# Four idle matmuls ahead of the second projection, in place of two ahead of the second and two ahead of the third

## The chip, the cores and the metric

The kernel runs on one NeuronCore of a Trainium2 chip. The metric is the device time of one execution in microseconds; the kernel before takes 975.07 us, the median of three runs (974.72 to 975.36).

## What is computed

Random-feature attention for 8 batches of 8 heads (576 tokens, 64 dimensions, 128 features), then a two-layer network with a softplus between (512 to 2048 to 512) over the 4608 tokens:

```python
def phi(x):
    proj = np.einsum('bhsd,md->bhsm', x, omega)
    sq = np.sum(x * x, axis=-1, keepdims=True) / 2.0
    h = proj - sq
    h = h - np.max(h, axis=-1, keepdims=True)
    return np.exp(h) / np.sqrt(m)
q_p, k_p = (phi(q_s), phi(k_s))
kv = np.einsum('bhsm,bhsd->bhmd', k_p, v)
z = np.sum(k_p, axis=2)
num = np.einsum('bhsm,bhmd->bhsd', q_p, kv)
den = np.einsum('bhsm,bhm->bhs', q_p, z)[..., None] + 1e-06
...
h = x @ w_in
g = np.maximum(h, 0.0) + np.log1p(np.exp(-np.abs(h)))
return (g @ w_out).astype(np.float32)
```

## The kernel before

The work is cut into *works*, one for each step on one engine: a load, the squares of a unit, its projection, its maxima, its bias, its exponentials, a product. A *unit* is one or two tiles of 128 tokens of a *quad* (four heads of one batch). The list `ORDER`, written out in the code, says in which order the works go to the engines, and each engine then runs its own part of that order strictly in a row; semaphores hold an instruction until what it reads has been made and what it overwrites has been read.

The change lies in the first microseconds, in the units of the first batch, keys first. One unit goes like this. SyncE issues its load (L664, tile `xk`). ScalarE squares it (L674; later GpSimd, L676) and VectorE sums the squares (L681). TensorE projects it on `omf` (L691): four float32 products on 64 rows each, of two of the heads in one bank and the other two in a second, which the profile shows as eight matmuls. VectorE takes the maxima of each bank (L739), and two short steps make the bias from maxima and squares (L746, L751). ScalarE makes the exponentials from the banks and the bias (L759), which frees the banks. The exponentials are the stationary side of the products with the values (L908, tile `kt`). In names such as `ppk_1_0_0` the first two numbers are the quad and the unit, the third the bank. The first five projections in their order on TensorE are 0_0, 1_0, 0_1, 1_1 and 0_2.

On VectorE the order of the units is interlaced: the bias of 0_0 (L751) stands behind the maxima of 1_0 (L739), and the bias of 1_0 behind the maxima of both banks of 0_1.

*Idle matmuls* are products whose result nobody reads. `fill` (L1779) makes n of them: each takes a 128x128 bfloat16 view of the unit matrix as weights and streams it four times, 512 columns, into a bank. Six, of a tile of zeros, stand at the start of TensorE's order, ahead of the first projection. The dictionary `early_` (L1784) gives for the works of mode "r" (the projections of the first batch), from the second on, how many idle matmuls go ahead of each; they write the first bank that the projection itself will write, so the projection waits until the last of them has been drained. A projection without idle matmuls ahead has no such wait. Later in the kernel there are no idle matmuls, and the order of the works doesn't depend on `early_`.

Of the kernel before, what the change touches and what calls it, by code (L numbers as in the profile page):

```python
# [464 lines left out]
def favor_softplus_kernel(ctx, tc, q0, k0, qx, kx, tx, vv, om, wi, wo, out):  # L465
# [49 lines left out]
    works, saves = [], []  # L515
# [1265 lines left out]
        for _ in range(n):  # L1781
            nc.tensor.matmul(t, x, x.unsqueeze(1).broadcast_to([P, 4, P]), start=True, stop=True)

    early_ = dict(zip([id(w) for w in works if w.mode == "r"][1:], (2, 2, 1, 1)))  # L1784
    with tc.manual_schedule():
        fill("at.0", 6, idle)
        out_, held = in_order(works, room)
# [107 lines left out]
```

## Time and profile before

| | |
|---|---|
| median of three runs | 975.07 us (974.72 to 975.36) |
| the profiled execution | 979.14 us |
| its span, first to last instruction | 977.4 us |
| TensorE busy | 967.2 us, 99% |
| VectorE busy | 783.2 us, 80% |
| ScalarE busy | 681.5 us, 70% |

All rows come from the one profiled execution. Times are microseconds from the start of its span. PE is the matmul side of TensorE and PEld its weight loads, DVE is VectorE, ACT ScalarE, POOL GpSimd. Each row of a timeline is a run of like instructions of one line; the number behind the start is the time from the start of the first to the end of the last, and what stands in brackets is how long the engine was idle ahead of it and what ended that. Matmuls overlap, so that the ends of one row and the start of the next can cross.

### The profile page before, as it was taken

To read this page: it belongs to the slowest core of one execution; us is meant where nothing else is said; L and a number is where in the kernel's file an instruction comes from. 1 tells how busy PE (TensorE), PEld (TensorE's weight loads), DVE (VectorE), ACT (ScalarE), POOL (GpSimd) and SP (SyncE) were. 2 spreads that over 40 slices of the span, in tenths; PEclk is the share of its full clock that TensorE was granted. 3 is DMA by queue.
4 is the path that set the end of the run, shared out by engine and by line. 5 is a ranking of instruction groups with operands and counts; after the bars stand their busy time and mean duration, and the time that the engine had idled before them with its cause. 6 is when DMAs were issued, how large, how long until landed. Compare 5 with 4: busy or idle time off the path is not lost.

```text
span 977.4 us, 17669 instructions
## 1 busy us (share of the span) xinstructions
PE 967.2 (99%) x5503; PEld 789.5 (81%) x5503; DVE 783.2 (80%) x2755; ACT 681.5 (70%) x1686; POOL 310.7 (32%) x282
## 2 busy tenths in 40 slices
PE   9999999999999999999999999999999999999998
PEld 6888888888788878888888887888888777888886
DVE  7999988887888788886988887888787778988610
ACT  6999976768576876877695677867586665766720
POOL 1344442323144341125442353333424212322100
PEclk9999999999999999999999999999999999999999
DMA  9877355444333433543343434432532511000002
GB/s 338 327 264 248 109 151 149 130 129 124 108 102 94 119 108 109 149 129 101 109 136 102 110 100 137 128 112 87 154 101 67 149 47 44 1 1 1 1 11 75
DMA packets 65116, 113.85 MB, mean 116 GB/s; under 512 B 18376, under 2 KB 38016, under 8 KB 65024
## 3 DMA queue, kind: packets, MB, share of 16 engines
q1 hardware_dynamic: 64720, 112.54, 36.8%
q8 instruction: 44, 0.72, 0.3%
q14 instruction: 48, 0.39, 0.1%
q10 hardware_dynamic: 304, 0.20, 0.1%
HBM read 85.68 MB, written 27.03 MB: 115 GB/s over the span
## 4 chain that ended last, share of the span: by engine, by line
PE 71%; DVE 2%; DMA 1%; issue 0%; ACT 0%; ACTq 0%; DVEq 0%
PE acc L1316 11%; PE acc L1317 11%; PE acc L1318 11%; PE h L1256 7%; PE h L1257 7%; PE h L1258 7%; PE pb L1596 3%; PE xp L1185 2%; PE pa L1596 2%; PE pc L1596 2%; PE ppk L716 2%; PE ppq L716 2%; PE kt L857 1%; PE ku L857 1%; DMA fdq<-flq 1%
## 5 line engine op out<-in xcount | busy, mean ns | idle before, releaser
L1316 PE MATMUL acc<-wo,gh 128*128 128x512 f32 x512 | 204.3, 399 | 0.0
L1317 PE MATMUL acc<-wo,gh 128*128 128x512 f32 x512 | 200.7, 392 | 0.0
L1318 PE MATMUL acc<-wo,gl 128*128 128x512 f32 x512 | 199.6, 390 | 0.0
L1256 PE MATMUL h<-xh,wi 128*128 128x512 f32 (+1 forms) x512 | 188.9, 369 | 0.0
L1257 PE MATMUL h<-xl,wi 128*128 128x512 f32 (+1 forms) x512 | 186.4, 364 | 0.0
L1258 PE MATMUL h<-xh,wi 128*128 128x512 f32 (+1 forms) x512 | 185.6, 363 | 0.0
L1279 POOL TENSOR_TENSOR gl<-u,gh 128x512 fp32r<-128x512 f32 (+1 forms) x75 | 88.9, 1186 | 227.9 <-ACT gh L1275 150.3
L1316 PEld LDWEIGHTS acc<-wo,gh 128*128 128x128 f32 x512 | 96.3, 188 | 23.1 <-issue 7.4
L1318 PEld LDWEIGHTS acc<-wo,gl 128*128 128x128 f32 x512 | 96.2, 188 | 21.0
L1256 PEld LDWEIGHTS h<-xh,wi 128*128 128x128 f32 x512 | 96.5, 188 | 18.3 <-DVE u L1271 1.5
L1262 ACT ACTIVATE u<-h 128x512 f32<-128x512 f32 (+1 forms) x128 | 70.7, 553 | 57.5 <-PE h L1258 41.9
L1258 PEld LDWEIGHTS h<-xh,wi 128*128 128x128 f32 x512 | 96.5, 188 | 15.7
L1317 PEld LDWEIGHTS acc<-wo,gh 128*128 128x128 f32 x512 | 96.6, 189 | 14.4
L1257 PEld LDWEIGHTS h<-xl,wi 128*128 128x128 f32 x512 | 96.7, 189 | 13.6
L1271 DVE SCALAR_TENSOR_TENSOR u<-h,u 128x512 f32<-128x512 f32 (+1 forms) x128 | 79.0, 617 | 28.8 <-ACT u L1268 26.8
L1265 ACT ACTIVATE u<-u 128x512 f32<-128x512 f32 (+1 forms) x128 | 75.3, 589 | 1.8
L1268 ACT ACTIVATE u<-u 128x512 f32<-128x512 f32 (+1 forms) x128 | 74.8, 585 | 1.8
L736 ACT ACTIVATE phk<-phk,smk 128x128 f32<-128x128 f32 x208 | 68.7, 393 | 4.4 <-DVE smk L751 4.1
L1094 DVE CUSTOM_DVE_ANT_0 junk<-phq,zb 128x128 uint8<-128x128 f32 (+1 forms) x228 | 68.7, 334 | 1.2 <-ACT phq L759 0.6
L1103 POOL TENSOR_TENSOR phq<-phq,dnq 128x512 f32<-128x512 f32 (+1 forms) x39 | 42.2, 1088 | 80.8 <-DVE dnq L1099 73.2
L736 ACT ACTIVATE phq<-phq,smq 128x128 f32<-128x128 f32 x194 | 62.5, 393 | 7.1 <-DVE smq L751 7.1
L731 DVE CUSTOM_DVE_ANT_0 phk<-ppk,phk 128x128 f32<-128x128 f32 x208 | 51.4, 285 | 12.6 <-ACT phk L726 11.2
(213 smaller groups left out, 2020.3 us busy)
## 6 DMA issues: line engine op xcount, KB each, us to landing
xk<-kx SPq DMA_DIRECT2D x28, 512.0 KB, 3.5
xq<-qx SPq DMA_DIRECT2D x28, 512.0 KB, 3.7
fdq<-flq SPq DMA_DIRECT2D x28, 512.0 KB, 3.2
qq<-fdq SPq DMA_DIRECT2D x112, 128.0 KB, 3.1
rawi<-wi SPq DMA_DIRECT2D x16, 512.0 KB, 6.9
rawo<-wo SPq DMA_DIRECT2D x16, 512.0 KB, 6.2
out<-o SPq DMA_DIRECT2D x32, 256.0 KB, 3.9
v<-vv SPq DMA_DIRECT2D x14, 576.0 KB, 4.3
```

The lines of the kernel that those rows point to most:

```text
L736: nc.scalar.activation(x, x, AF.Exp, bias=b["sm"][:, 2, c : c + 1])
L1256: nc.tensor.matmul(b["h"], wh, xh[:, cc, t], start=cc == 0, stop=False)
L1257: nc.tensor.matmul(b["h"], wh, xl[:, cc, t], start=False, stop=False)
L1258: nc.tensor.matmul(b["h"], wl, xh[:, cc, t], start=False, stop=cc == NCC - 1)
L1262: nc.scalar.activation(b["u"], b["h"], AF.Abs)
L1265: nc.scalar.activation(b["u"], b["u"], AF.Exp, scale=-1.0)
L1268: nc.scalar.activation(b["u"], b["u"], AF.Ln, bias=1.0)
L1271: nc.vector.scalar_tensor_tensor(b["u"], b["h"], 0.0, b["u"], ALU.max, ALU.add)
L1279: (nc.vector if e == "DVE" else nc.gpsimd).tensor_tensor(b["gl"], b["u"], b["gh"].bitcast(F32), ALU.subtract)
L1316: nc.tensor.matmul(dst, gh, w2[fc][:, 0, c], start=start, stop=False, **kw)
L1317: nc.tensor.matmul(dst, gh, w2[fc][:, 1, c], start=False, stop=False, **kw)
L1318: nc.tensor.matmul(dst, gl, w2[fc][:, 0, c], start=False, stop=stop, **kw)
```

## The change

The four numbers of `early_` are those of the second to the fifth projection.

```diff
-    early_ = dict(zip([id(w) for w in works if w.mode == "r"][1:], (2, 2, 1, 1)))
+    early_ = dict(zip([id(w) for w in works if w.mode == "r"][1:], (4, 0, 1, 1)))
```

TensorE, just behind the first projection: two idle matmuls, the second projection, two idle matmuls (a weight load and a matmul each). Before:

```order
L1782 LDWEIGHTS ident
L1782 MATMUL fill<-ident 128x512
L1782 LDWEIGHTS ident
L1782 MATMUL fill<-ident 128x512
L691 MATMUL ppk_1_0_0_125<-omf,xk_1_0_103 128x128
L691 MATMUL ppk_1_0_1_126<-omf,xk_1_0_103 128x128
L691 MATMUL ppk_1_0_0_125<-omf,xk_1_0_103 128x128
L691 MATMUL ppk_1_0_1_126<-omf,xk_1_0_103 128x128
L1782 LDWEIGHTS ident
L1782 MATMUL fill<-ident 128x512
L1782 LDWEIGHTS ident
L1782 MATMUL fill<-ident 128x512
```

Then comes the third projection. In the changed program two idle matmuls stand ahead of these rows already, and the two below are the third and fourth; the second projection and the third follow:

```order
L1782 LDWEIGHTS ident
L1782 MATMUL fill<-ident 128x512
L1782 LDWEIGHTS ident
L1782 MATMUL fill<-ident 128x512
L691 MATMUL ppk_1_0_0_127<-omf,xk_1_0_103 128x128
L691 MATMUL ppk_1_0_1_128<-omf,xk_1_0_103 128x128
L691 MATMUL ppk_1_0_0_127<-omf,xk_1_0_103 128x128
L691 MATMUL ppk_1_0_1_128<-omf,xk_1_0_103 128x128
L691 MATMUL ppk_0_1_0_145<-omf,xk_0_1_105 128x128
L691 MATMUL ppk_0_1_1_146<-omf,xk_0_1_105 128x128
L691 MATMUL ppk_0_1_0_145<-omf,xk_0_1_105 128x128
L691 MATMUL ppk_0_1_1_146<-omf,xk_0_1_105 128x128
```

The second projection has moved behind two more idle matmuls, and the third stands right behind it. The idle matmul ahead of the fourth projection comes next in both.

VectorE, from the maxima of the second projection on, in the changed program; in the program before these rows are the same but for the numbers of buffers (`smk_1_0` and the banks of the second projection):

```order
L739 TENSOR_REDUCE smk_1_0_135<-ppk_1_0_0_127 128x2
L739 TENSOR_REDUCE smk_1_0_135<-ppk_1_0_1_128 128x2
L751 SCALAR_TENSOR_TENSOR smk_0_0_116<-smk_0_0_116 128x4
L681 TENSOR_REDUCE smk_0_1_156<-xk_0_1_105 128x4
L739 TENSOR_REDUCE smk_0_1_156<-ppk_0_1_0_145 128x2
L746 SCALAR_TENSOR_TENSOR smk_1_0_135<-smk_1_0_135 128x4
L739 TENSOR_REDUCE smk_0_1_156<-ppk_0_1_1_146 128x2
L751 SCALAR_TENSOR_TENSOR smk_1_0_135<-smk_1_0_135 128x4
```

Nothing has moved there: the bias of 0_0 (the L751 of `smk_0_0`) still waits behind both maxima of the second projection. The orders of ScalarE, GpSimd and SyncE are the same as well.

## Rows read from the trace of the kernel before

**Rows 1.** The page, busy us by engine (share of the span) x instructions.

```profile
PE 967.2 (99%) x5503; PEld 789.5 (81%) x5503; DVE 783.2 (80%) x2755; ACT 681.5 (70%) x1686; POOL 310.7 (32%) x282
```

**Rows 2.** The page, the span in 40 slices, busy tenths.

```profile
PE   9999999999999999999999999999999999999998
...
PEclk9999999999999999999999999999999999999999
DMA  9877355444333433543343434432532511000002
```

**Rows 3.** Timeline of TensorE, 3.5 to 24 us: start, us, operation, count, idle before.

```profile
4.95 1.04 PE L1782 MATMUL fill<-ident 128*128 128x512 bf16 x2
6.05 1.23 PE L691 MATMUL ppk<-omf,xk 64*128 64x128 f32 x8
7.21 1.04 PE L1782 MATMUL fill<-ident 128*128 128x512 bf16 x2
8.30 1.23 PE L691 MATMUL ppk<-omf,xk 64*128 64x128 f32 x8
9.46 0.45 PE L1782 MATMUL fill<-ident 128*128 128x512 bf16 x1
9.96 0.71 PE L691 MATMUL ppk<-omf,xk 64*128 64x128 f32 x8
...
12.14 0.71 PE L691 MATMUL ppk<-omf,xk 64*128 64x128 f32 x6 [0.15 <-ACT xk L759]
12.78 1.11 PE L908 MATMUL kt<-xk 128*128 128x65 f32 x8
...
19.56 0.71 PE L691 MATMUL ppq<-omf,xq 64*128 64x128 f32 x8
...
21.68 1.16 PE L691 MATMUL ppq<-omf,xq 64*128 64x128 f32 x16
```

**Rows 4.** The fill tile, whole span: durations in ns, least/median/most.

```profile
L1782 PE MATMUL fill<-ident x6: 390/609/634, 5.0 to 10.6; 128*128 128x512 bf16 x6
```

**Rows 5.** Windows: length, busy of PE, PEld, DVE, ACT, POOL, granted clock, DMA.

```profile
1.00:9.60 8.60, 8.42 (x35) 3.90 (x35) 3.21 (x13) 3.91 (x9) 0.29 (x1) 1.00 0.86 276
9.60:20.00 10.40, 10.10 (x89) 8.24 (x89) 9.94 (x41) 8.52 (x32) 2.66 (x5) 1.00 1.04 397
20.00:60.00 40.00, 39.03 (x352) 34.59 (x348) 39.48 (x140) 39.82 (x121) 15.10 (x14) 1.00 0.85 319
60.00:300.00 240.00, 237.88 (x1553) 197.07 (x1553) 209.77 (x729) 186.37 (x495) 89.09 (x82) 1.00 0.47 145
```

**Rows 6.** Timeline of VectorE, 3.5 to 13 us.

```profile
7.30 0.76 DVE L739 TENSOR_REDUCE smk<-ppk 128x2 f32<-128x256 f32 x2 [0.94 <-PE ppk L691]
7.98 0.15 DVE L751 SCALAR_TENSOR_TENSOR smk<-smk 128x4 f32<-128x4 f32 x1
8.04 0.42 DVE L681 TENSOR_REDUCE smk<-xk 128x4 f32<-128x256 f32 x1
9.56 0.42 DVE L739 TENSOR_REDUCE smk<-ppk 128x2 f32<-128x256 f32 x1 [1.10 <-PE ppk L691]
```

**Rows 7.** Timeline of ScalarE, 3.5 to 13 us.

```profile
5.43 0.42 ACT L674 ACTIVATE xk<-xk 128x256 f32<-128x256 f32 x1 [1.36 <-DMA xk<-k]
6.18 0.42 ACT L674 ACTIVATE xk<-xk 128x256 f32<-128x256 f32 x1 [0.34 <-DMA xk<-k]
8.22 0.63 ACT L759 ACTIVATE xk<-ppk,smk 128x128 f32<-128x128 f32 x2 [1.62 <-DVE smk L751]
...
9.04 0.63 ACT L759 ACTIVATE xk<-ppk,smk 128x128 f32<-128x128 f32 x2
10.64 0.63 ACT L759 ACTIVATE xk<-ppk,smk 128x128 f32<-128x128 f32 x2 [0.98 <-DVE smk L746]
```

**Rows 8.** Waits of 0 to 16 us: sum, times, longest.

```profile
PEld ppk L691 <- PE fill L1782: 3.6, 5, 1.0
```

**Rows 9.** Waits of TensorE, whole span.

```profile
PE ppq L716 <- DVE spq L709: 1.6, 2, 1.3
```

## The prediction

> **What bounds the kernel now.** I read the busy times first. TensorE works 967.2 us of a span of 977.4 us, against 783.2 for VectorE and 681.5 for ScalarE [rows 1]; only 10.2 us of the whole span are without a matmul, so the kernel is bound by TensorE, and whatever makes its stream start later or earlier has a chance to reach the end. The slices say that the transfers are dense in the first tenth only (9, 8, 7, 7 tenths of the DMA engines) [rows 2]. The change lies in the first 10 us, so the next view is the timeline of TensorE there [rows 3]. The reader is to see two things in it. First, the stream is a row of idle matmuls and projections with hardly a wait: up to the 0.15 us at 12.14 each group starts where the one before it ends. Second, the groups get shorter: a projection of eight matmuls takes 1.23 us at 4 to 9 us and 0.71 us at 9.96, and the idle matmul at 9.46 takes 0.45. The view of the fill tile gives 609 to 634 ns for one idle matmul early and 390 for the last [rows 4]. [...] So TensorE ran at the low level up to about 9.6 us and at the high one after. The granted clock is shown as 1.00 from the start [rows 5]; it can't be read there ahead of the first recorded change, and the durations decide.
>
> Then the two engines that use the projections. VectorE waits 0.94 us for the second projection and 1.10 us for the third [rows 6]; ScalarE waits 1.62 us ahead of its first exponentials and 0.98 us ahead of those at 10.64 [rows 7]. So from 5 to 10.6 us the path runs projection, maxima, bias, exponentials. From 9.6 to 20 us VectorE is busy 9.94 of 10.40 us, and from 20 to 60 us ScalarE 39.82 of 40 [rows 5]: from there on those two set the pace of the first block, and TensorE waits for ScalarE at 12.14 [rows 3].
>
> **The change, part by part: TensorE.** The changed program has the same number of idle matmuls ahead of the third projection, four; all four now stand ahead of the second one. Two more there cost 2 x 0.43 = 0.86 us [rows 3, 4], and nothing hides them: the second projection's load had landed by 5.43, when ScalarE took it up [rows 7], so it starts at 6.05 + 0.86 = 6.91 and ends at 6.91 + 1.23 = 8.14 in place of 7.28. The third follows it without idle matmuls. Eight matmuls behind eight others add 1.16 - 0.71 = 0.45 us at the high level [rows 3]; at the low one between 0.45 x 1.23 / 0.71 = 0.78 and twice 0.45 = 0.90, an estimate. Its load had landed by 6.18 [rows 7]. It ends at 8.92 to 9.04, in place of 8.30 + 1.23 = 9.53: the hand-over that is gone (a projection waits for the last idle matmul to drain before it loads weights) saves TensorE 0.5 to 0.6 us. The fourth and the fifth projection, their one idle matmul each and all that follows are unchanged; the fourth starts 0.5 us earlier.
>
> **VectorE and ScalarE, at the same clock.** The order on VectorE is the same as before, and this is where the delay of the second projection costs: the bias of the first unit (L751) stands behind the maxima of the second projection (L739). Those maxima move from 7.30 to 8.16, the bias from 7.98 to 8.84, the next reduce from 8.04 to 8.90, ending at 9.32 [rows 6]. The third projection's maxima, which came at 9.56, can begin at 9.32: 0.24 us earlier. ScalarE's first exponentials move from 8.22 to 9.08. From there to its exponentials at 10.64 it has 10.64 - 0.98 - 8.22 = 1.44 us of work [rows 7], so these come at 10.52, 0.12 us earlier. ScalarE is the later of the two, so the delay eats nearly all that the removed hand-over saves: 0.86 lost, 0.98 of waiting filled. TensorE's own 0.5 us are hidden, as it waits for ScalarE at 12.14 anyway. **At the same clock the change is worth 0.1 us.**
>
> **The clock.** What can be worth more is where the level rises. Before it rose, TensorE had three times changed over between idle matmuls and a projection, and its weight loads waited 0.96 us each time [rows 3, 8]. In the changed program the stretch from 4.95 to about 6.8 us is one row of 512-column matmuls, followed by two projections with no change-over between. I take it that the level rises in or just behind the four idle matmuls, at 6.2 to 7 us; no row of before shows that, it is my choice. The last idle matmul then adds about half of 0.43, 0.21, so that the row ends near 6.6; the second projection takes 0.71 and ends at 7.4, as before (7.28), and the third ends at 7.4 + 0.45 = 7.85. Now VectorE and ScalarE lose nothing at the start: ScalarE's first exponentials stay at 8.22 to 8.4, and those of 10.64 come at 8.3 + 1.44 = 9.74 to 9.85. **Gain 0.8 us** on the pace of the first block. Its ends: 0.1 us, if the level rises no earlier, and 1.8 us, if the whole stretch from 6.0 to 9.6 were worth half its length, which ScalarE's own work of 1.44 us from 8.22 excludes.
>
> [...]
>
> **How much of it reaches the end.** TensorE's longest wait in the whole span is 1.3 us, and its waits for other engines sum to a few us [rows 9]. A gain dies at a wait for something that doesn't move with it, a load above all; a delay passes on. Between all of 0.8 and nothing I take the half, 0.4: from 60 us on TensorE is busy 237.88 of 240 us [rows 5], which speaks for passing on, but the loads of the first 100 us are dense [rows 2], which speaks against. The profiled execution took 979.14 us; the sum gives 979.14 - 0.4 = 978.7 there. It lies 4.07 us above the median of the runs shown, 975.07, from which I subtract the same 0.4: **974.7 us**. With 0.2% of 975 us, 1.95 us, as the least that a measurement here tells from no change, this is no change.
>
> **Rivals.** (1) The level rises where it did, at about 9.6 us. For it: TensorE did nearly the same amount of work up to there, and had been busy since 0.99 us without a rise. [...] It gives the 0.1 us of the sum at the same clock: 974.95. (2) The rise comes later, and the kernel is slower. In place of idle matmuls between the second and third projection stand short matmuls on 64 rows, in two groups back to back; if these hold the clock down, the low level lasts to about 13.2 us. TensorE then does in the 3.6 us after 9.6 what takes it 1.8 at the high level; it had gained 0.5, so it is 1.3 us late at most. What ScalarE and VectorE hide of that is between nothing and two thirds: 0.4 to 1.3 us slower, 975.5 to 976.4. Slower by more than 0.2% needs a low level up to about 16.6 us: 3.5 us of loss less 0.5 and less a hidden 1.05 is 1.95, 977.0. Against it: the fourth and the fifth projection still have their idle matmuls, and from 12.78 on matmuls on 128 rows stand between the projections [rows 3]. (3) The rise isn't the program's: it moves from run to run, and the change does nothing. The three runs lie 0.64 us apart, less than the price of a rise some us earlier or later, which speaks against. The time would be 975.1, with 0.8 us on either side. [...]
>
> **Chances.** Forecast 0.45, rival 1 0.32, rival 2 0.14, rival 3 0.09. Forecast and rivals 1 and 3 lie within 0.2% whole, the forecast even with its full 0.8 us (974.3). Of rival 2, 0.05 lies above 977.0 us; 0.03 I leave for a gain over 1.95 us, which no step here gives. So faster 0.03, same 0.92, slower 0.05. The range goes from 973.6 (the full 0.8 and the 0.6 us that runs lie apart) to 976.2 (nearly all of rival 2 at 13.2 us).
>
> **What would show it.** In the profile of the changed kernel: four idle matmuls from 4.95 us; the second projection at 6.9 if the level stayed low, near 6.65 if it rose; eight matmuls in 0.71 us for the third projection (or two projections in about 1.2) if it rose, 2.0 to 2.1 if not; ScalarE's first exponentials at 9.1 or near 8.3; the exponentials of the second unit at 10.5 or 9.8. The forecast is wrong if projections of eight still take 1.23 us after 9.6 us, or if the span changes by more than 2 us with these places as forecast, which would mean that TensorE's waits behind 20 us answer to the start in a way that the rows don't show.

## The result, and the profile after

The changed kernel takes 984.29 us, the median of 21 runs, against 975.32 us of the kernel before in 21 runs beside them; the ratio is 1.0052 with a 95% interval of 1.0032 to 1.0071. The median tells little here, because the runs of the changed kernel fall into two groups with hardly anything between: eight runs at 975.2 to 976.2 us and two more at 977.6 and 979.4, all with a mean granted clock (the clock that TensorE is granted, as a share of full speed, over the run) of 0.997 to 1.00, and eleven at 984.3 us and above (ten within 984.29 to 984.58, one at 988.5), with a granted clock of 0.987 or less. The two groups' medians are 975.79 and 984.39. The 21 runs of before reach from 974.7 to 979.2. The forecast was 974.7, within 973.6 to 976.2.

The profiled execution of the changed kernel (984.57 us, span 982.8) belongs to the upper group. Of its page, the first line and the slices, which answer to [rows 1, 2]:

```profile
PE 974.8 (99%) x5503; PEld 798.2 (81%) x5503; DVE 784.3 (80%) x2755; ACT 682.0 (69%) x1686; POOL 309.8 (32%) x282
...
PE   9999999999999999999999999999999999999998
...
PEclk7799999999999999999999999999999999999999
```

TensorE is busy 974.8 us, 7.6 us more than in [rows 1], with the same 5503 matmuls, so some of them took longer. Which ones, the clock line says: it reads 7 of 10 in the first two slices of 24.6 us each, and 9 everywhere else. The timeline of TensorE in the first 20 us answers to [rows 3] (start, length, operation, count, idle ahead):

```profile
4.94 1.31 PE L1782 MATMUL fill<-ident 128*128 128x512 bf16 x4
6.31 1.16 PE L691 MATMUL ppk<-omf,xk 64*128 64x128 f32 x16
...
8.65 0.38 PE L1782 MATMUL fill<-ident 128*128 128x512 bf16 x1
9.08 1.39 PE L691 MATMUL ppk<-omf,xk 64*128 64x128 f32 x10
10.81 0.71 PE L691 MATMUL ppk<-omf,xk 64*128 64x128 f32 x6 [0.34 <-ACT xk L759]
11.45 1.16 PE L908 MATMUL kt<-xk 128*128 128x65 f32 x8
12.54 1.23 PE L691 MATMUL ppk<-omf,xk 64*128 64x128 f32 x8
13.70 1.97 PE L908 MATMUL kt<-xk 128*128 128x65 f32 x8
15.60 1.65 PE L691 MATMUL ppk<-omf,xk 64*128 64x128 f32 x12
```

The four idle matmuls stand at 4.94 and take 1.31 us, not the 1.9 of four at the low level (0.61 for the first and 1.04 - 0.61 = 0.43 for each of three more [rows 3, 4]) and not the 1.02 of four at the high one (at 8.43 us with (4, 0, 1, 4), below). So the level rose in the middle of them, at about 5.5 us, an estimate from these lengths, where before it rose at 9.6. The second and the third projection take 1.16 us together, all at the high level. So far this is the forecast. Then come the fifth and the sixth projection. Ten matmuls at 9.08 take 1.39 us, though eight take 0.71 at the high level and sixteen 1.16 [rows 3], which makes about 0.8 for ten: TensorE waits within the row, and again 0.34 us for ScalarE at 10.81. Behind that, the projection at 12.54 takes 1.23 us again, and the products with the values 1.97 at 13.70 in place of 1.11 at 12.78 [rows 3]. **The level has fallen back.** The windows give the stretch (length, busy of PE, PEld, DVE, ACT and POOL, granted clock, DMA):

```profile
0.00:12.36 12.36, 10.72 (x68) 6.27 (x68) 7.44 (x32) 6.92 (x22) 2.54 (x9) 1.00 0.84 296
12.36:36.26 23.90, 23.90 (x133) 21.84 (x133) 15.69 (x59) 14.49 (x47) 3.34 (x4) 0.50 1.04 401
36.26:100.00 63.74, 62.96 (x536) 54.47 (x536) 62.16 (x192) 62.98 (x178) 27.54 (x26) 1.00 0.64 226
```

The 1.00 of the first row says nothing of the time ahead of 5.5 us, in which the level was low by the durations. From 12.36 to 36.26 us the granted clock is 0.50, half of full speed. TensorE is busy for all of the 23.90 us and gets 133 matmuls done. VectorE and ScalarE, busy nearly throughout in the same part of the kernel before [rows 5], work 15.69 and 14.49 of 23.90 us: at the low level TensorE is the engine that holds the first block back.

### The profile page after: what moved, and what is told of

It reads as the page before. It is cut to its first block, busy times and chain, and to the rows that moved or that the text cites. A ratio compares the mean times of both kernels' runs of the same rounds, so it can differ in the third digit from the quotient of the medians.

```text
span 982.8 us, 17668 instructions
## 1 busy us (share of the span) xinstructions
PE 974.8 (99%) x5503; PEld 798.2 (81%) x5503; DVE 784.3 (80%) x2755; ACT 682.0 (69%) x1686; POOL 309.8 (32%) x282
## 4 chain that ended last, share of the span: by engine, by line
PE 94%; DVE 3%; ACT 2%; issue 1%; ACTq 0%; DVEq 0%
PE acc L1316 14%; PE acc L1317 13%; PE acc L1318 13%; PE h L1256 10%; PE h L1257 10%; PE h L1258 10%; PE xp L1185 3%; PE pb L1596 3%; PE ppk L716 3%; PE ppq L716 2%; PE pa L1596 2%; PE pc L1596 2%; PE kt L857 2%; PE kt L908 1%; PE ku L857 1%; PE ppk L691 1%
## 5 line engine op out<-in xcount | busy, mean ns | idle before, releaser
L1256 PE MATMUL h<-xh,wi 128*128 128x512 f32 (+1 forms) x512 | 188.9, 369 | 0.0
L1256 PEld LDWEIGHTS h<-xh,wi 128*128 128x128 f32 x512 | 96.4, 188 | 18.4 <-DVE u L1271 1.6
```

What stands on the lines that cost most here:

```text
L1256: nc.tensor.matmul(b["h"], wh, xh[:, cc, t], start=cc == 0, stop=False)
```

## The experiments

Every experiment changes one thing, the four numbers of `early_`, some with more numbers for the later projections. They ran on four chips, each group beside the kernel before; the changed kernel was run again in one group. Theory F (falls back): the early rise lets TensorE run ahead of ScalarE; while it waits for banks at 9 to 11 us the level falls, and the matmuls of the first block at the low level don't raise it again before 36 us. Theory P (path): the second projection comes later, and what is late is the path through VectorE and ScalarE, not the clock.

**The kernel before, again**, for a second profile.

> The kernel before, unchanged, for a second profile of it. Theory F (the clock falls back): the rise of the level differs from run to run; an ordinary run of about 975.3 us has its rise earlier than the 9.6 us of the first profile (which took 979.1), and no fall before the end. Rival P (the path through VectorE and ScalarE, no clock): the rise lies at about 9.6 us again and the time at 975 to 979 us has nothing to do with it.

975.46 us, the median of 8 runs (974.79 to 977.05); its profiled execution took 974.79. TensorE:

```profile
3.79 0.76 PE L691 MATMUL ppk<-omf,xk 64*128 64x128 f32 x8
4.48 0.60 PE L1782 MATMUL fill<-ident 128*128 128x512 bf16 x2
5.66 0.72 PE L691 MATMUL ppk<-omf,xk 64*128 64x128 f32 x8 [0.58 <-DMA xk<-k]
...
9.16 0.78 PE L691 MATMUL ppk<-omf,xk 64*128 64x128 f32 x8
10.16 0.80 PE L691 MATMUL ppk<-omf,xk 64*128 64x128 f32 x8 [0.21 <-ACT xk L759]
10.89 1.11 PE L908 MATMUL kt<-xk 128*128 128x65 f32 x8
11.93 0.71 PE L691 MATMUL ppk<-omf,xk 64*128 64x128 f32 x8
```

The first projection takes 0.76 us and the first pair of idle matmuls 0.60: the level rose by about 4 us here, where the profile that the prediction rests on has 9.6. That execution, at 979.14, was one of the slowest that the kernel before has given: of its 153 runs in all these comparisons 118 lie below 977 us and five above 979.1, the slowest at 981.25. So the point of the rise moves from run to run. But the early rise is not all of the 4.35 us between the two executions. In the first profile the first product of the first layer (L1256) starts at 39.82 us, 2.15 us later than in the second (37.67, below), and at 264 us TensorE waits for VectorE there, 0.35 and 1.29 us, the longest wait of [rows 9]; the second profile has no such wait:

```profile
39.82 0.39 PE L1256 MATMUL h<-xh,wi 128*128 128x256 f32 x1
```

```profile
263.98 0.38 PE L716 MATMUL ppq<-omr,spq 128*128 128x256 f32 x1 [0.35 <-DVE spq L709]
265.65 0.39 PE L716 MATMUL ppq<-omr,spq 128*128 128x256 f32 x1 [1.29 <-DVE spq L709]
```

One profile of (2, 0, 1, 1), a kernel below, has a late rise as well (a projection at 8.71 us still takes 1.23 us) but no such wait, and it took 975.43 us. In the second profile the waits at the fifth and sixth projection are there too (0.80 us for eight at 10.16 and 0.21 us idle), but short: from 9.16 to the first product with the values at 10.89 it is 1.73 us, in the changed kernel 2.37 (9.08 to 11.45). The level stays high; 218 matmuls are done in the stretch in which the changed kernel did 133:

```profile
12.36:36.26 23.90, 23.05 (x218) 20.41 (x215) 23.32 (x91) 23.26 (x74) 6.08 (x8) 1.00 1.04 401
```

The first product of the first layer starts at 37.67 us here and at 47.44 in the changed kernel, 9.8 us later, and the profiled executions end 984.57 - 974.79 = 9.8 us apart: the whole difference is made before 47 us and handed on to the end unchanged.

```profile
37.67 0.39 PE L1256 MATMUL h<-xh,wi 128*128 128x256 f32 x1
```

```profile
47.44 0.39 PE L1256 MATMUL h<-xh,wi 128*128 128x256 f32 x1
```

**Idle matmuls where TensorE waits, and none at all.** First the changed kernel with four in place of one ahead of the fifth projection, then a kernel with none ahead of the second to fifth.

```diff
-(4, 0, 1, 1)
+(4, 0, 1, 4)
```

> The changed kernel with four idle matmuls in place of one ahead of the fifth projection, where TensorE waits for ScalarE from 9.5 to 10.8 us in the profile of after. Theory F: the wait is filled with matmuls, the level does not fall at 12.4 us, all runs at 975 to 977 us. Rival P: three more idle matmuls on the same path, 0.2 us each: bimodal as after, most runs at 984 to 985 us.

```diff
-(4, 0, 1, 1)
+(0, 0, 0, 0)
```

> No idle matmuls ahead of the second to fifth projection. Theory F: the level rises late or falls back at once and stays low until the dense products of the first layer, past 30 us; 984 to 990 us in most runs, which is the price of the low level. Rival P: the second projection comes 0.9 us earlier than before, nothing is delayed; 974 to 976 us.

The first: 975.66 us, 11 runs of 975.12 to 979.04, none at 984; ratio to before 1.0001 (0.9991 to 1.0011). Three more idle matmuls remove a loss of 9 us, which P can't explain. They fill the wait:

```profile
8.43 1.02 PE L1782 MATMUL fill<-ident 128*128 128x512 bf16 x4
9.51 0.93 PE L691 MATMUL ppk<-omf,xk 64*128 64x128 f32 x10
10.60 0.71 PE L691 MATMUL ppk<-omf,xk 64*128 64x128 f32 x6 [0.15 <-ACT xk L759]
11.23 1.11 PE L908 MATMUL kt<-xk 128*128 128x65 f32 x8
```

The wait for ScalarE is 0.15 us, and from the fifth projection at 9.51 to the first product with the values at 11.23 it is 1.72 us, as long as in the kernel before (1.73). The second: 985.17 us, the median of six runs, one at 975.80 and five of 984.11 to 988.99; ratio 1.0090 (1.0055 to 1.0126). Nothing is delayed in it by an idle matmul; TensorE waits 1.51 us and 0.53 us ahead of the fifth and the sixth projection, a projection takes 1.23 us again at 12.92, and the windows show the low level for 23.89 us from 11.38 on:

```profile
5.48 2.12 PE L691 MATMUL ppk<-omf,xk 64*128 64x128 f32 x24 [0.63 <-DMA xk<-k]
9.11 0.81 PE L691 MATMUL ppk<-omf,xk 64*128 64x128 f32 x8 [1.51 <-DVE smk L739]
10.44 0.81 PE L691 MATMUL ppk<-omf,xk 64*128 64x128 f32 x8 [0.53 <-DVE smk L751]
11.18 1.81 PE L908 MATMUL kt<-xk 128*128 128x65 f32 x8
12.92 1.23 PE L691 MATMUL ppk<-omf,xk 64*128 64x128 f32 x8
```

```profile
11.38:35.27 23.89, 23.89 (x132) 21.83 (x132) 15.08 (x57) 13.65 (x45) 4.57 (x6) 0.50 1.04 401
```

So it matters where the idle matmuls stand: with three more of them where TensorE would wait, the level stayed up (granted clock 1.00 from 5.10 to 15.34 us in the profile). One of the five longer runs of the second kernel, 985.76 us, has a granted clock of 0.999. A low level from the start on would read like this, as it reads 1.00 in the first row of [rows 5], but no profile shows that run.

**Raising the level again.** The changed kernel with two idle matmuls ahead of each of the sixth to eleventh projection, and one with four ahead of the eighth and four ahead of the ninth alone, that is from 14 us on, behind the fall.

```diff
-(4, 0, 1, 1)
+(4, 0, 1, 1, 2, 2, 2, 2, 2, 2)
```

> The changed kernel with two idle matmuls ahead of each of the sixth to eleventh projection besides. Theory F: where the level falls at 12 us it rises again by about 20 us, and in most runs it doesn't fall; 976 to 980 us. Rival P: twelve more idle matmuls of 0.2 to 0.43 us on the path: 987 to 989 us in the runs that took 984.

```diff
-(4, 0, 1, 1)
+(4, 0, 1, 1, 0, 0, 4, 4)
```

> The changed kernel with four idle matmuls ahead of the eighth and four ahead of the ninth projection besides (15 to 18 us). Theory F (the level falls at about 12.4 us in some runs, and the thin products of the first block can't raise it again before 36 us): the fall stays, but the level is high again by about 20 us; two groups, 976 to 977 us and 979 to 981 us, none at 984. Rival P (the loss is not the low level): the slow group stays at 984 us or above, as eight idle matmuls come on top.

With twelve spread out, seven runs of 977.58 to 978.69 us and no second group: 2.6 us slower than before, the price of the matmuls, but none at 984. The first two of the twelve stand ahead of the sixth projection, in the wait, so this kernel doesn't tell a fall that was prevented from one that was undone. With eight behind the fall, the runs split as forecast: seven of 976.54 to 977.83 us with a granted clock of 0.999 to 1.00, and five of 979.85 to 981.20 with 0.994 to 0.996. The fall is still there, but it costs about 3 us, not 9. A mean granted clock of 0.996 over 978 us is (1 - 0.996) x 2 x 978 = 8 us at half the clock, and 0.994 is 12, against 24 in the changed kernel. No profile shows one of the five, but their clock and time bear out both parts of F: the loss goes with the length of the low level, and in the changed kernel the first block didn't end it before 36 us.

**The two halves of the change, each alone, and the changed kernel once more.**

> The changed kernel once more, for the share of its two times and for a second profile. Theory F: the runs fall into two groups again, 975 to 976 and 984 to 985 us, and the granted clock of the run tells which (1.00 and 0.987). Theory P without the clock would leave one group.

```diff
-(2, 2, 1, 1)
+(2, 0, 1, 1)
```

> Half of the change alone: the two idle matmuls ahead of the third projection are gone, none added ahead of the second. Theory F in its form 'TensorE gets ahead of ScalarE once the third projection follows the second at once': two groups as after, many runs at 984 to 985 us. Rival G (the four in one piece do it, by the early rise or the later second projection): one group at 975 to 976 us.

```diff
-(2, 2, 1, 1)
+(4, 2, 1, 1)
```

> The other half alone: two more idle matmuls ahead of the second projection, those ahead of the third stay. Theory F: TensorE is 0.4 us later at the fifth projection than in the changed kernel and waits less there: one group, 975 to 977 us. Rival G: two groups, as the four in one piece are there.

The changed kernel gives its two groups again, though in another share: nine runs of 974.75 to 976.10 us and three of 984.24 to 984.66; its median is 975.84 this time, and the ratio 1.0003 (0.998 to 1.0026) says nothing. Of all its 33 runs 14 lie at 984 us or above. Each half alone gives one group: twelve runs of 974.92 to 976.24 us with the removal, 0.9987 (0.9976 to 0.9998) of the kernel before, and twelve of 975.22 to 976.70 with the addition, 0.9991 (0.998 to 1.0001). The addition is as F forecast: with the idle matmuls ahead of the third projection kept, the fifth starts at 9.54, and both projections take 1.76 us without a break that the profile shows ahead of a row:

```profile
9.54 1.76 PE L691 MATMUL ppk<-omf,xk 64*128 64x128 f32 x16
```

The removal is not. F had said that it lets TensorE run ahead, and so it does: from 8.40 to the first product at 10.71 it is 2.31 us, about as long as in the changed kernel (2.37), and yet no run fell.

```profile
5.59 1.33 PE L691 MATMUL ppk<-omf,xk 64*128 64x128 f32 x16 [0.18 <-DMA xk<-k]
...
8.40 1.05 PE L691 MATMUL ppk<-omf,xk 64*128 64x128 f32 x8
9.67 1.11 PE L691 MATMUL ppk<-omf,xk 64*128 64x128 f32 x8 [0.22 <-DMA xk<-k]
10.71 1.11 PE L908 MATMUL kt<-xk 128*128 128x65 f32 x8
```

So the length of this stretch alone doesn't decide; F in that form is wrong. Nor is it the same wait throughout: the profile puts the 0.22 us ahead of the sixth projection down to its load, not to ScalarE.

**Four in a row elsewhere, and the dose.**

```diff
-(2, 2, 1, 1)
+(0, 4, 1, 1)
```

> The same four idle matmuls in one piece, ahead of the third projection in place of the second. Theory F: the second projection is early, so ScalarE starts earlier, and TensorE reaches the fifth projection as late as before; its wait there is short: one group, 975 to 976 us, with at most a run or two above. Rival G: as the changed kernel, two groups.

```diff
-(4, 0, 1, 1)
+(4, 0, 1, 2)
```

> The changed kernel with one more idle matmul ahead of the fifth projection. Theory F: 0.2 to 0.4 us of the wait of 1.2 us are filled; the slow group shrinks from about two in five runs to one in ten or none. Rival (any four in a row with the removed hand-over fall, whatever follows): as the changed kernel.

Four in one piece ahead of the third projection give twelve runs of 975.07 to 981.17 us (median 976.06, ratio 0.9996, 0.9981 to 1.0012), none in an upper group; it is not the row of four as such. One more idle matmul ahead of the fifth projection, in the changed kernel, leaves none of twelve runs at 984 (975.13 to 980.02).

> The kernel with two idle matmuls fewer, once more, on another chip if it comes so: 975.0 to 975.5 us, one group. Theory W (TensorE's wait at 8.6 to 10.7 us is nearly as long as in the changed kernel, so it can fall as well): one or two runs of twelve at 984 us. If not, the 0.4 us longer lead of the first exponentials decides.

```diff
-(2, 2, 1, 1)
+(2, 0, 1, 2)
```

> Two ahead of the second, none ahead of the third, one and two: the removal with one more idle matmul in TensorE's wait. Theory F: the wait hides it; one group, 975.0 to 975.6 us, no run above 976.5 us, and faster than before by 0.1%.

The removal alone, on another chip: eleven runs of 974.76 to 976.02, ratio 0.9996 (0.9987 to 1.0005). Over both chips 23 of 23 runs without a fall, and 0.04 to 0.13% below the kernel before; one of the two intervals holds 1. With one more idle matmul in the wait, forecast as safer still and 0.1% faster than before, the ratio is 1.0003 (0.9989 to 1.0018), and one run of eleven took 983.27 us with a granted clock of 0.990: a miss for F, which no profile of that run explains.

**The number ahead of the second projection, and the wait by itself.**

```diff
-(4, 0, 1, 1)
+(3, 0, 1, 1)
```

> Three idle matmuls ahead of the second projection, none ahead of the third. Theory F (the later second projection delays ScalarE by 0.43 us for each idle matmul at the low level, and TensorE's wait at the fifth and sixth grows with it): between two ahead (0 of 23 runs fell) and four (14 of 33): one to four runs of twelve at 983 to 985 us. Rival R (the row of exactly four ends on the rise by chance): as two ahead, none.

```diff
-(4, 0, 1, 1)
+(6, 0, 1, 1)
```

> Six idle matmuls ahead of the second projection, none ahead of the third. Theory F: TensorE itself comes later by the same idle matmuls as ScalarE, at the high level by then, so the wait doesn't grow past that of four: the share of runs at 984 to 986 us is like that of four, four to six of twelve, and the others lie at 976 us. Rival S (more idle matmuls always keep the level up): none at 984.

```diff
-(4, 0, 1, 1)
+(4, 0, 1, 0)
```

> The changed kernel without the one idle matmul ahead of the fifth projection, at which TensorE waits. Theory F: the wait is 0.4 us longer, six or more of twelve runs at 984 to 986 us. Rival R: as the changed kernel, three to six of twelve.

| ahead of the 2nd, 3rd, 4th, 5th | runs at 983 us or above | others |
|---|---|---|
| 2, 2, 1, 1 (before) | 0 of 153 | 974.7 to 981.3 |
| 2, 0, 1, 1 | 0 of 23 | 974.8 to 976.2 |
| 3, 0, 1, 1 | 1 of 11 | 974.9 to 979.7 |
| 4, 0, 1, 1 (after) | 14 of 33 | 974.8 to 979.4 |
| 6, 0, 1, 1 | 4 of 12 | 975.4 to 978.1 |
| 4, 0, 1, 0 | 8 of 12 | 975.9 to 976.5 |
| 0, 0, 0, 0 | 5 of 6 | 975.8 |
| 4, 0, 1, 2 | 0 of 12 | 975.1 to 980.0 |
| 4, 0, 1, 4 | 0 of 11 | 975.1 to 979.0 |
| 2, 0, 1, 2 | 1 of 11 | 974.8 to 975.9 |
| 0, 4, 1, 1 | 0 of 12 | 975.1 to 981.2 |
| 4, 2, 1, 1 | 0 of 12 | 975.2 to 976.7 |

All three came out within what F had forecast. With two, three and four ahead of the second projection 0 of 23, 1 of 11 and 14 of 33 runs fell, with six 4 of 12. Without the idle matmul at the wait it was 8 of 12, with one more there 0 of 12, with three more 0 of 11. Eleven or twelve runs make a rough share, and the changed kernel itself gave 11 of 21 once and 3 of 12 the other time: the 1 of 11, the 4 and the 8 of 12 are in the order that F forecast, no more. The none of 23 with a fuller wait against 14 of 33 is the clear difference. In the profile of the last kernel TensorE waits for ScalarE twice, 0.34 us each, and the projection at 12.66 is at the low level again:

```profile
8.00 1.28 PE L691 MATMUL ppk<-omf,xk 64*128 64x128 f32 x10
9.61 1.00 PE L691 MATMUL ppk<-omf,xk 64*128 64x128 f32 x8 [0.34 <-ACT xk L759]
10.95 0.71 PE L691 MATMUL ppk<-omf,xk 64*128 64x128 f32 x6 [0.34 <-ACT xk L759]
11.59 1.14 PE L908 MATMUL kt<-xk 128*128 128x65 f32 x8
12.66 1.23 PE L691 MATMUL ppk<-omf,xk 64*128 64x128 f32 x8
```

What stays open is what decides in a single run. The kernel with the eight idle matmuls behind the fall has the four numbers of the changed kernel and the same instructions up to 14 us; its profile (977.56 us) is of a run that didn't fall, with the same wait:

```profile
4.99 1.56 PE L1782 MATMUL fill<-ident 128*128 128x512 bf16 x4
...
9.38 1.39 PE L691 MATMUL ppk<-omf,xk 64*128 64x128 f32 x10
11.11 0.71 PE L691 MATMUL ppk<-omf,xk 64*128 64x128 f32 x6 [0.34 <-ACT xk L759]
...
12.79 0.71 PE L691 MATMUL ppk<-omf,xk 64*128 64x128 f32 x8
```

From the fifth projection to the first product with the values it is 2.37 us here (9.38 to 11.75) as in the changed kernel (9.08 to 11.45), with the same 1.39 us for ten matmuls and the same 0.34 us behind them, and yet the projection at 12.79 takes 0.71 us, ahead of any of the eight: the level stayed up. So a fuller wait made a fall rarer from kernel to kernel, but a wait like this is not enough for a fall. What the two profiles show to differ up to there is where the level rose: the four idle matmuls take 1.31 us in the changed kernel and 1.56 here, so that it rose later, and what follows comes 0.3 us later. Whether that decides, two executions can't show; nor is it shown why (2, 0, 1, 1) never fell and one run of (2, 0, 1, 2) did.

## Why the prediction was wrong

**The work on TensorE and the clock's rise: right, and early.** The level rose in the four idle matmuls, as chosen, at 5.5 us (forecast 6.2 to 7). That it rose there because of the row of four, no run shows: in its second profile the kernel before had its rise by about 4 us without that row. Nor does a row of before show that the low level is half of the high one, on which the forecast's 0.21 us for the last idle matmul rests; the profile of the changed kernel does, with its 0.50 from 12.36 us on. The second and third projection were done at 6.31 + 1.16 = 7.47 us, forecast 7.85. ScalarE, answering to [rows 7]:

```profile
7.97 0.63 ACT L759 ACTIVATE xk<-ppk,smk 128x128 f32<-128x128 f32 x2 [1.46 <-DVE smk L751]
...
8.79 1.14 ACT L759 ACTIVATE xk<-ppk,smk 128x128 f32<-128x128 f32 x4
...
10.10 2.73 ACT L759 ACTIVATE xk<-ppk,smk 128x128 f32<-128x128 f32 x10
```

The first exponentials came at 7.97 (forecast 8.22 to 8.4), and the second unit's, the last two of the four from 8.79 on, well before the forecast 9.74. At the first product with the values TensorE was 1.33 us ahead of the profile that the forecast rests on (11.45 against 12.78 in [rows 3]), more than the 0.8 us of the forecast. Then came what the prediction had named as its sign of being wrong: a projection of eight took 1.23 us again, at 12.54.

**The step that failed** is the one that called TensorE's waits free: "TensorE's own 0.5 us are hidden, as it waits for ScalarE at 12.14 anyway". The sum took a wait of TensorE as a place where gains end, and the level, once high, as given. The runs showed that this wait can have a price of its own: TensorE stood with holes at 9.1 to 10.8 us, the level fell at 12.36, and 24 us at half the clock cost about 9 us (the medians of the two groups lie 8.6 us apart here and 9.0 in the second set of runs). That happened in 14 of 33 runs, and in none of 23 with one or three more idle matmuls in the wait. That the median landed in the upper group is chance, 11 of 21 runs here against 3 of 12 there; that there is such a group is the change's doing. No rival had a fall after the rise; rival 2 had a late rise; the 13.2 us up to which its low level lasts are a supposition that no run shows, and it was priced to 16.6 us at the most. The right price of a low level in the first block, up to 36 us, stood in no row that I had read.

**The base was wrong as well.** The prediction saw that the profiled execution took 979.14 us, 4.07 more than the median, and subtracted it. What made that execution long it did not ask. Of the 4.35 us by which it is longer than that of the second profile, 2.15 were made ahead of the first layer, where the second profile has the level rise by 4 us, and 1.64 by the waits at 264 us, of which [rows 9] had the longest. In the second profile the first product with the values starts at 10.89 us, 0.56 us ahead of the changed kernel's 11.45: there the gain of an earlier rise was in the kernel before already. That this holds for most of its runs, and so for the median of 975.07, is likely, but one profile doesn't show it. Rival 3, that the rise moves from run to run, was right on that, and got 0.09. Runs of the changed kernel that don't fall take 974.8 to 976.2 us for the most part, no better than before: the gain that the forecast saw is not there.

**Passing on.** The prediction took the half of its gain as reaching the end; for a delay the runs showed all of it: 9.8 us at 37 to 47 us, 9.8 us at the end. In 15 of the 17 profiles the time of the execution is 937.0 to 937.8 us more than the start of the first L1256. The two others are the first profile of before (939.3) and that of (4, 0, 1, 2) (941.0), and both have the wait of 1.3 us at about 264 us.

## What to carry to other kernels

A wait of TensorE is not always free: in this kernel whether 9 us were lost went, from kernel to kernel, with what stood in one wait. Ask of a change that makes TensorE faster in one place whether it will then stand with holes in the next, and try the idle matmuls where it waits, not only where it is late. Where one profiled execution differs from the median of the runs by more than the change can be worth, find out what is different in that execution before summing on it; several times of one kernel and the granted clock of each run tell more than one trace. A change whose runs split into two groups is judged by the share of each, and a median over them can land in either.

## What the runs showed of the hardware

The low level, once it had come back, ended only at 35 to 36 us: the granted clock was 0.50 for 23.9 us in the upper group's profiles (12.36 to 36.26 in the changed kernel, 11.38 to 35.27 without idle matmuls), although the profile counts TensorE as busy for all of it. In the profile of the changed kernel it came back this once: from 36.26 us to the end of the span the granted clock is 1.00. With eight more idle matmuls in that stretch the runs that fell spent about 8 to 12 us at the low level, by their mean clock. And once, in the kernel with two idle matmuls ahead of the fifth projection, the clock dropped in the middle of the kernel: the granted clock was 0.51 from 265.7 to 269.2 us in an execution of 980.02 us, and back at 1.00 after. Ahead of that drop stand the waits for VectorE that the first profile of the kernel before has too, at 1.00 throughout (263.98 and 265.65 us above). Here as well the same waits were followed by a fall in one execution and by none in another:

```profile
263.25 0.39 PE L716 MATMUL ppq<-omr,spq 128*128 128x256 f32 x1 [0.40 <-DVE spq L709]
264.93 0.38 PE L716 MATMUL ppq<-omr,spq 128*128 128x256 f32 x1 [1.28 <-DVE spq L709]
```

```profile
265.70:269.20 3.50, 3.50 (x12) 2.90 (x11) 2.37 (x15) 0.38 (x1) 0.00 (x0) 0.51 0.65 178
```
